# Decode attention and MLP on one core: weight products in VectorE and ScalarE loops, 451 TensorE instructions for 812, one load per contiguous 8 MB

## The chip, the cores and the metric

The kernel runs on one core of one Trainium2 chip. The metric is the device time of one execution in microseconds. Runs of one kernel agree closely: the kernel before took 1303.3, 1303.55 and 1303.74 us.

## What is computed

One decode step for one token: a layer norm, attention of 32 query heads over 8 cached key/value heads with 65536 keys each, a ReLU MLP beside it, and their sum with the input. All arrays are float32. The caches hold 2 x 268 MB, the weights 24 MB; each byte is read once.

```python
D, Hq, Hkv, Sk, Dh, Dff = 512, 32, 8, 65536, 128, 1792
xn = _layernorm(x, axis=-1)
q = (xn @ wq) as 32 heads of 128
scores = einsum("bhqd,bhkd->bhqk", q, repeat(k, 4)) * Dh ** -0.5
o = einsum("bhqk,bhkd->bhqd", softmax(scores), repeat(v, 4))
return x + o.reshape(1, 1, 4096) @ wo + relu(xn @ w1) @ w2
```

## The kernel before

**Loads.** SyncE (SP) issues all the large loads on one queue, in this order: wq in two pieces (4 and 28 slices; a slice is 128 x 512 floats, 256 KB) into the buffer `vs`, then 64 loads of 8.4 MB each, keys into `ks` and values into `vs` by turns (k0 v0 k1 v1 ... k31 v31), then w1 and w2 into `ks`, then wo in seven pieces into `vs`. There is one buffer each for keys and values. So k(i+1) is issued when the scores of step i have left `ks` (semaphore `k_free`, L297 behind L375), and v(i+1) when the weighted sum of step i has left `vs` (`v_free`, L302 behind L398). The first value load waits until TensorE has read wq out of `vs` (L310). In HBM the 128 rows of such a load, 64 KB each, lie 256 KB apart for keys and values alike; w1 and w2 are read in whole contiguous arrays.

**Head.** VectorE makes the layer norm, with two small matmuls that sum over partitions (L202 to L222). TensorE multiplies 32 slices of wq by selectors of x into one PSUM bank (L280); a copy, four transposes and a sum give the queries `qall`. GpSimd (POOL) copies four of them at a time to `qcur`.

**Steps.** 32 steps (8 heads of 4). In each, TensorE makes scores of 16384 keys with 32 matmuls (L344), VectorE transposes them from PSUM (L376), takes a running maximum (L385 to L393), ScalarE exponentiates (L422), and TensorE sums values by weights with 32 matmuls (L360). VectorE adds that to `acc` with the correction `alpha` (L400 or L402). A float32 matmul stands as two weight loads and two matmuls in the records. After four steps VectorE folds the head into `fin` (L408 to L415), and POOL copies it to `fins`.

**Tail.** After the last step TensorE multiplies w1 (L443), collects the heads (L453, L458), and transposes; VectorE builds the weights `hT` and `sw` (L460 to L494). TensorE then multiplies 14 slices of w2 and 28 of wo into four rows of `acc_z` (L505), as they land. `rows` takes `acc_z` (L536). The last four slices of wo go straight to `acc_y` (L540), `rows` is added there (L525), VectorE transposes (L552), and SP writes the 512 results (L561).

**Names.** `Flow.op` adds a wait and a semaphore increment to an instruction; the wait is then an instruction of its own only where it is not carried by the operation. `load_slices` issues one load for each count in a list. `nc.Fori` is a loop run by the engine's own sequencer, without unrolling. `mark_branch_hint_location` and `branch_hint` place a branch prefetch hint: before, on VectorE.

Of the kernel before, what the change touches and what calls it, by code (L numbers as in the profile page):

```python
# [15 lines left out]
P = 128  # L16
# [9 lines left out]
CHUNK = SK  # L26
# [3 lines left out]
NP = TPC // NT  # L30
# [6 lines left out]
WQ = [4, 28]  # L37
WO = [8, 8, 8, 4, 2, 1, 1]
PAIRED = 16
DIRECT = 28  # L40
# [29 lines left out]
def attention_and_mlp_kernel(  # L70
# [35 lines left out]
    def bank(name, *shape):  # L106
        return nc.alloc_psum_tensor(name, [P, *shape], F32).ap()

    ks = place("ks", NT * KEYS)
    vs = place("vs", NT * KEYS)  # L110
    tr = place("tr", NT * SUB, 32)
    wt = place("wt", NT * SUB, G)
    xT, xc, sq, xn = (place(n, A) for n in ("xT", "xc", "sq", "xn"))
    x4, yt = place("x4", P), place("yt", 32, 4)
    sw = place("sw", SLICES)
    mine = place("mine", HKV)
    octet = place("octet", P)
    eighth = place("eighth", R)

    flat_tr = tr.rearrange("p b i -> p (b i)")  # L120
    xs = flat_tr[:, : SLICES * HKV].rearrange("p (i h) -> p i h", h=HKV)
    xm = flat_tr[:, SLICES * HKV : SLICES * (HKV + 1)]
    om, spread = flat_tr[:, : R * HQ], flat_tr[:, R * HQ : 2 * R * HQ].rearrange("p (r h g) -> p r h g", r=R, h=HKV)
    heads = flat_tr[:, 2 * R * HQ : 2 * R * HQ + 2 * DH]
    st = place("st", 8)
# [4 lines left out]
    qall, qcur = place("qall", HKV, G), place("qcur", 32)  # L130
# [7 lines left out]
    acc, masked = place("acc", WIDE, DH), place("masked", WIDE, DH)  # L138
    fin, fins = place("fin", DH + G), place("fins", HKV, DH + G)
    rows = place("rows", 512)  # L140
    total, oT, hT = place("total", HQ), place("oT", HQ), place("hT", 4 * CT)

    pa, pb = bank("pa", 2, TW), bank("pb", 2, TW)
    acc_o, acc_z, acc_y, pm = (bank(n, 512) for n in ("acc_o", "acc_z", "acc_y", "pm"))

    names = "k_in v_in tiles scores m_out bias_out a_out w_out o_out k_free v_free q_in d_out f_out f_free"
    (
        k_in, v_in, s_tiles, s_dve, s_max, s_bias, s_alpha, s_w, s_o,
        k_free, v_free, q_in, s_diff, f_out, f_free,
    ) = (nc.alloc_semaphore(n) for n in names.split())  # L150
    PE, DV, AC, GP = (Flow(nc, e, n) for e, n in ((te, "pe"), (ve, "dve"), (se, "act"), (ge, "pool")))
# [6 lines left out]

    def load_slices(name, src, counts):
        marks = []  # L160
        for n in counts:
            cut = slice(len(marks) * D, (len(marks) + n) * D)
            marks += [load(sy, f"{name}{len(marks)}", vs[:, cut], src[:, cut])] * n
        return marks


    with tc.tile_critical():
        x_in = load(se, "x_in", xT, x.rearrange("(p a) -> p a", p=P))
        wq_in = load_slices("wq", wq.rearrange("h (i r) a f -> (h i) (r a f)", r=R), WQ)
        sy.dma_start(ks, k[0, 0, :, : NT * KEYS]).then_inc(k_in, 16)  # L170
# [4 lines left out]
    make_identity_marks = []  # L175

# [3 lines left out]
    d = memset(DV, ones, 1.0)  # L180
    d = memset(DV, x4, 0.0)
    x4_free = DV.mark
    d = memset(DV, qcur, 0.0)
    for t in (acc_o, acc_z, pm):
        memset(DV, t, 0.0)
    memset(DV, acc_y[:, :P], 0.0)

# [9 lines left out]
    x4_in = None  # L197
    se.wait_ge(*x4_free)
    x4_in = load(se, "x4_in", x4[0:P:32, :], x.rearrange("(c n) -> c n", c=CT))


    DV.op(lambda e: e.reduce_sum(st[:, 0:1], xT, axis=AX.X), x_in)  # L202
    PE.op(lambda e: e.matmul(pm[:, 0:1], ones, st[:, 0:1], start=True, stop=True), DV.mark)
    DV.op(lambda e: e.tensor_scalar_mul(st[:, 1:2], pm[:, 0:1], 1.0 / D), PE.mark)
    DV.op(lambda e: e.tensor_scalar(xc, xT, st[:, 1:2], None, op0=ALU.subtract), DV.mark)
    DV.op(lambda e: e.tensor_mul(sq, xc, xc), DV.mark)
    DV.op(lambda e: e.reduce_sum(st[:, 2:3], sq, axis=AX.X), DV.mark)
    PE.op(lambda e: e.matmul(pm[:, 1:2], ones, st[:, 2:3], start=True, stop=True), DV.mark)
    DV.op(
        lambda e: e.tensor_scalar(st[:, 3:4], pm[:, 1:2], 1.0 / D, EPS, op0=ALU.mult, op1=ALU.add),  # L210
        PE.mark,
    )
# [3 lines left out]
    AC.op(lambda e: e.activation(alpha[:, 0:1], st[:, 3:4], AF.Exp))  # L216
# [5 lines left out]
    xn_in = DV.op(lambda e: e.tensor_scalar_mul(xn, xc, st[:, 7:8]), DV.mark)  # L222
# [14 lines left out]
    DV.op(lambda e: e.reduce_sum(mine, ident.rearrange("p (h i) -> p h i", h=HKV), axis=AX.X))  # L237
    DV.op(lambda e: e.reduce_sum(eighth, ident.rearrange("p (i r) -> p r i", r=R), axis=AX.X))
    DV.op(lambda e: e.reduce_sum(octet[:, : P // R], ident.rearrange("p (i r) -> p i r", r=R), axis=AX.X))
    DV.op(  # L240
        lambda e: e.tensor_copy(
            octet[:, P // R :].rearrange("p (h i) -> p h i", i=P // R),
            octet[:, : P // R].unsqueeze(1).to_broadcast([P, HKV - 1, P // R]),
        ),
        DV.mark,
    )
    DV.op(
        lambda e: e.tensor_mul(
            xm.rearrange("p (r a) -> p r a", a=A),
            eighth.unsqueeze(2).to_broadcast([P, R, A]), xn.unsqueeze(1).to_broadcast([P, R, A]),  # L250
        )
    )
    pz = pb[:, 1, :]
    PE.op(lambda e: e.matmul(pz[:, :SLICES], octet, xm, start=True, stop=True), DV.mark)
    xs_in = DV.op(
        lambda e: e.tensor_mul(
            xs, pz[:, :SLICES].unsqueeze(2).to_broadcast([P, SLICES, HKV]),
            mine.unsqueeze(1).to_broadcast([P, SLICES, HKV]),
        ),
        PE.mark,  # L260
    )
    DV.op(lambda e: e.memset(idg, 1.0))
    DV.op(lambda e: e.tensor_copy(idg[:, :G], ident[:G, :G]), DV.mark)

    pr, pt = pa[:, 0, :], pb[:, 0, :]

    def turn():

        for j in range(4):
            PE.op(  # L270
                lambda e: e.transpose(pt[:, j * P : (j + 1) * P], rows[:, j * P : (j + 1) * P], ident),
                DV.mark, made,
            )
        return pt.rearrange("p (j c l) -> p j c l", j=4, c=CT)

    cleared = DV.op(lambda e: e.memset(pr, 0.0))
    for i in range(SLICES):
        c = i % CT
        PE.op(
            lambda e: e.matmul(  # L280
                pr[32 * c : 32 * c + HKV, :], xs[:, i, :], vs[:, i * 512 : (i + 1) * 512],
                start=(i < CT), stop=(i >= SLICES - CT),
            ),
            cleared, xs_in, wq_in[i],
        )
    wq_read = PE.mark
    DV.op(lambda e: e.tensor_copy(rows, pr), PE.mark)
    q = turn()[:, :, :, :HKV].rearrange("p j c h -> p h j c")
    DV.op(lambda e: e.reduce_sum(qall, q, axis=AX.X), PE.mark)
    q_made = DV.mark  # L290
    PE.need(DV.mark)
    AC.need(DV.mark)


    def k_load(h, n):
        sy.wait_ge(k_free, 1).then_inc(k_free, -1)
        sy.dma_start(ks, k[h, 0, :, n * NT * KEYS : (n + 1) * NT * KEYS]).then_inc(k_in, 16)  # L297

    def v_load(h, n):
        sy.wait_ge(v_free, 1).then_inc(v_free, -1)  # L300
        src = v[h].rearrange("(p t b) d -> p t (b d)", p=P, b=SUB)
        sy.dma_start(vs, src[:, n * NT : (n + 1) * NT, :].rearrange("p t f -> p (t f)")).then_inc(v_in, 16)  # L302

    def head(h):
        v_load(h, 0)
        for n in range(1, NP):
            k_load(h, n)
# [285 lines left out]
```

## Time and profile before

| | |
|---|---|
| median of 3 runs | 1303.55 us |
| profiled execution, its own time | 1303.26 us |
| span of its instructions | 1301.9 us |
| what lies around the span | 1.36 us |
| busy: TensorE / VectorE / ScalarE | 664.9 / 268.4 / 76.0 us |
| moved by DMA | 561.06 MB |

The span begins with the first instruction and ends with the last. Lines "L344" are line numbers of the kernel. In a timeline the columns are start, duration, engine, line, operation, output<-inputs, count, and in brackets how long the engine stood idle before and what released it. In a table of groups they are the shape, the count, total busy time and mean ns of one, then idle time before. "SPq" is SP's queue, that is an instruction that issues a DMA or waits; "PEq" and "DVEq" are the same of TensorE and VectorE. Register, branch and semaphore instructions have no rows.

### The profile page before, as it was taken

The page shows a single profiled execution, that of the slowest core. Times are in us where ns is not written, and L with a number is a line of the kernel's source. Part 1 is how long each engine was busy: PE and PEld are TensorE (multiplying, and loading weights), DVE is VectorE, ACT ScalarE, POOL GpSimd, SP SyncE. Part 2 cuts the span into 40 slices and gives each one's busy share as a digit, 9 for nine tenths or more (in the row PEclk, how much of TensorE's full clock was granted, in tenths as well). Part 3 has the DMA queues.
Part 4 walks back from the last instruction along what each step waited for, and adds up shares of the span by engine and source line. Part 5 has one row for each costly group of instructions (what it writes and reads, how often), then busy time and mean ns, then how long its engine had stood idle before and what let it go on. Part 6 is the DMA issues. An engine that isn't in the chain of part 4 may idle for free. (4 is left out here: it accounts for less than half of the span.)

```text
span 1301.9 us, 10665 instructions
## 1 busy us (share of the span) xinstructions
PE 664.9 (51%) x4512; PEld 185.6 (14%) x4512; DVE 268.4 (21%) x398; ACT 76.0 (6%) x292; POOL 4.1 (0%) x22
## 2 busy tenths in 40 slices
PE   3355356455446445545545545544544644544658
PEld 1111111111111111111111111111111111111112
DVE  2221122221122222012222012222112222201222
ACT  0000000000000000000000000000000000000000
POOL 0000000000000000000000000000000000000000
PEclk9776676777677677667677677768777767767769
DMA  9999999999999999999999999999999999999998
GB/s 419 419 449 419 451 419 445 425 427 443 421 449 421 449 419 451 419 445 425 431 439 425 445 421 449 419 451 419 445 425 435 435 425 445 421 449 421 449 416 361
DMA packets 11101, 561.06 MB, mean 431 GB/s; under 512 B 1492, under 2 KB 1496, under 8 KB 1880
## 3 DMA queue, kind: packets, MB, share of 16 engines
q1 hardware_dynamic: 10944, 561.00, 99.7%
q8 instruction: 3, 0.05, 0.0%
q10 hardware_dynamic: 152, 0.00, 0.0%
q14 instruction: 2, 0.02, 0.0%
HBM read 560.99 MB, written 0.00 MB: 431 GB/s over the span
## 5 line engine op out<-in xcount | busy, mean ns | idle before, releaser
L360 PE MATMUL acc_o<-vs,wt 128*16 128x512 f32 x2048 | 296.3, 743 | 179.0 <-PEq L356 179.0
L344 PE MATMUL pa<-ks,qcur 128*32 128x512 f32 x1024 | 176.5, 822 | 323.8 <-PEq L339 323.8
L376 DVE STREAM_TRANSPOSE tr<-pa 128x1024 f32<-128x1024 f32 x64 | 80.0, 1250 | 412.9 <-PE pa L344 412.9
L344 PE MATMUL pb<-ks,qcur 128*32 128x512 f32 x1024 | 139.5, 665 | 0.0
L422 ACT ACTIVATE wt<-tr,bias 128x128 f32<-128x128 f32 x128 | 64.3, 511 | 1084.5 <-ACTq L420 1084.5
L360 PEld LDWEIGHTS acc_o<-vs,wt 128*16 128x16 f32 x2048 | 69.6, 114 | 379.0 <-issue 379.0
L344 PEld LDWEIGHTS pa<-ks,qcur 128*32 128x32 f32 x1024 | 38.9, 134 | 431.4 <-issue 422.4
L402 DVE SCALAR_TENSOR_TENSOR acc<-acc,alpha,acc_o 128x512 f32<-128x512 f32 x24 | 17.9, 747 | 353.2 <-PE acc_o L360 353.2
L376 DVE STREAM_TRANSPOSE tr<-pb 128x1024 f32<-128x1024 f32 x64 | 80.0, 1250 | 49.6 <-PE pb L344 49.6
L344 PEld LDWEIGHTS pb<-ks,qcur 128*32 128x32 f32 x1024 | 41.9, 132 | 107.8 <-issue 88.6
L349 PE MATMUL pm<-ident,m 128*4 128x128 f32 x32 | 10.3, 320 | 87.7 <-DVE m L388 67.2
L400 DVE COPY acc<-acc_o 128x512 f32<-128x512 f32 x8 | 5.5, 692 | 121.5 <-PE acc_o L360 121.5
L350 PE MATMUL pm<-dg,ones 4*128 4x4 f32 x64 | 15.4, 309 | 21.4 <-DVE dg L392 21.4
L385 DVE TENSOR_REDUCE mc<-tr 128x4 f32<-128x512 f32 x24 | 24.1, 1006 | 1.8
L422 ACT ACTIVATION_READ_ACCUMULATOR wt<-tr,bias 128x1 f32 x128 | 23.9, 187 | 0.0
L349 PEld LDWEIGHTS pm<-ident,m 128*4 128x4 f32 x32 | 2.6, 81 | 116.7 <-DVE m L388 89.0
L350 PEld LDWEIGHTS pm<-dg,ones 4*128 4x128 f32 x64 | 12.6, 245 | 29.0 <-DVE dg L392 29.0
L351 PE MATMUL pm<-dg,rowg 4*128 4x1 f32 x64 | 14.7, 296 | 0.0
L280 PE MATMUL pa<-vs,tr 128*8 128x512 f32 x64 | 9.6, 754 | 8.7 <-DMA vs<-wq 7.4
L351 PEld LDWEIGHTS pm<-dg,rowg 4*128 4x128 f32 x64 | 13.4, 258 | 0.0
L390 DVE TENSOR_REDUCE mg<-pm 4x1 f32<-4x128 f32 x32 | 8.9, 279 | 13.2 <-PE pm L349 13.2
L505 PE MATMUL acc_z<-vs,sw 128*1 128x512 f32 x56 | 10.1, 592 | 2.1 <-DMA vs<-wo 2.1
(98 smaller groups left out, 97.8 us busy)
## 6 DMA issues: line engine op xcount, KB each, us to landing
vs<-wq SPq DMA_DIRECT2D x1, 7168.0 KB, 21.3
ks<-w SPq DMA_DIRECT2D x2, 3584.0 KB, 22.4
vs<-wo SPq DMA_DIRECT2D x3, 2048.0 KB, 16.4
vs<-wq SPq DMA_DIRECT2D x1, 1024.0 KB, 4.8
vs<-wo SPq DMA_DIRECT2D x1, 1024.0 KB, 22.8
ks<-k SPq DMA_DIRECT2D x32, 28.8
vs<-v SPq DMA_DIRECT2D x32, 28.9
vs<-wo SPq DMA_DIRECT2D x1, 512.0 KB, 23.6
```

The source lines that it names most:

```text
L280: lambda e: e.matmul(pr[32 * c : 32 * c + HKV, :], xs[:, i, :], vs[:, i * 512 : (i + 1) * 512], start=(i < CT), stop=(i >= SLICES - CT),),
L344: i = te.matmul(tile_of[32 * c : 32 * c + 32, :], qcur, ks[:, at : at + TW], start=True, stop=True)
L349: te.transpose(pm[:G, :P], m, ident)._wait_ge(s_dve, 3).then_inc(s_max, 1)
L350: te.matmul(pm[:, P : P + G], ones[:G, :], dg[:, :G], start=True, stop=True)._wait_ge(s_dve, 4)
L351: te.matmul(pm[:, P + G : P + G + 1], rowg, dg[:, G : G + 1], start=True, stop=True).then_inc(s_max, 1)
L360: mm = te.matmul(acc_o[32 * c : 32 * c + WIDE * G, :], wt[:, i * WIDE : (i + 1) * WIDE, :].rearrange("p b g -> p (b g)"), vs[:, i * 512 : ...
L376: i = ve.transpose(tr[:, s * SUB : (s + 2) * SUB, :].rearrange("p b i -> p (b i)"), (pa, pb)[s // 2 % 2].rearrange("p i k -> p (i k)"),)._ ...
L385: i = ve.reduce_max(top, tr[:, :, :G].rearrange("p b g -> p g b"), axis=AX.X)
L390: ve.reduce_max(mg, pm[:G, :P], axis=AX.X)._wait_ge(s_max, 1)
L402: ve.scalar_tensor_tensor(flat, flat, alpha[:, n : n + 1], acc_o, op0=ALU.mult, op1=ALU.add)
L422: i = se.activation(wt[:, :, g], tr[:, :, g], AF.Exp, bias=bias[:, n, g : g + 1], scale=scale, accum_out=part[:, n, g : g + 1],)
L505: lambda e: e.matmul(acc_z[32 * c : 32 * c + 1, :], lhsT, row, start=c not in begun, stop=last),
```

## The change

- **Layout.** `CHUNK` is 16384 keys instead of 65536. The 128 rows of each key or value load now lie back to back in HBM, 8.4 MB contiguous. Packet sizes stay 64 KB. SP's loads are one loop of 31 turns.
- **Head.** wq comes in two pieces of 16 slices; w1 is loaded right behind wq into a buffer of its own, ahead of the keys. The layer norm runs on 16 partitions with VectorE transposes instead of matmuls. wq is multiplied by VectorE, one slice per turn of a loop of 32 turns (L265 to L270): two waits, an address made in registers, and a SCALAR_TENSOR_TENSOR `accq = slice * xs + accq` that waits for the one before it through the semaphore `own`. One matmul with `mine` sums it per head. Then VectorE multiplies w1 in four instructions of 1792 elements (L315 to L322), and four matmuls and a transpose give the hidden values `hs`. TensorE waits for them (L334) ahead of the loop of steps. The first value load waits for the end of the wq loop (`q_dve`, L346).
- **Steps.** As before. In the fourth step of a head what does not need the last sum is folded ahead of it (L449 to L461). ScalarE, VectorE and POOL share one loop over heads.
- **Tail.** The last value load is split in two (21 and 11 of its 32 slices). Behind it come w2 in two pieces and wo in eight, `[9, 7, 5, 5, 3, 1, 1, 1]`; the first two pieces of wo fit in `ks` and need no `v_free`. Slices 0 and 1 of w2 are added by VectorE ahead of the loop; slices 2 to 39 of w2 and wo are taken in a loop of 19 turns, in which ScalarE scales an even slice and TensorE sums it over partitions, and VectorE adds an odd slice to `accy`. Slices 40 to 42 are matmuls into `acc_z`. `rows` is `accy + acc_z`; the last three slices go to `acc_y`.
- **TensorE's code.** 451 instructions instead of 812, and a branch prefetch hint ahead of its loop of steps, whose branch stands in a block that is never entered. VectorE's hint is gone.

```diff
-CHUNK = SK
+CHUNK = SK // 4
...
+    for n in range(2):
+        ge.wait_ge(*wq_in[n * SLICES // 2]).then_inc(go_dve, SLICES // 2)
...
+    with nc.Fori(0, SLICES, engines=[ENG.DVE]) as t:
+        ve.wait_ge(go_dve, 1).then_inc(go_dve, -1)
+        ve.wait_ge(own, 1).then_inc(own, -1)
+        ve.scalar_tensor_tensor(
+            accq, vs[:, bass.ds(t * D, D)], xs[:, bass.ds(t, 1)], accq, op0=ALU.mult, op1=ALU.add
+        ).then_inc(own, 1)
+    ve.wait_ge(own, 1).then_inc(q_dve, 1)
...
-    for i in range(SLICES):
-        c = i % CT
...
+    for a in range(A):
+        w = t1[:, a * DFF : (a + 1) * DFF]
+        if a == 0:
+            DV.op(lambda e: e.tensor_scalar_mul(h1, w, xn[:, 0:1]), DV.mark, w1_in)
+        else:
+            DV.op(
+                lambda e: e.scalar_tensor_tensor(h1, w, xn[:, a : a + 1], h1, op0=ALU.mult, op1=ALU.add), DV.mark
...
     PE.need(DV.mark)
...
+    sy.wait_ge(q_dve, 1)
     sy.sem_inc(v_free, 1)
+    with nc.Fori(0, STEPS - 1, engines=[ENG.SP]) as i:
+        v_load(i)
+        k_load(i + 1)
+    sy.wait_ge(v_free, 1).then_inc(v_free, -1)
+    sy.dma_start(vs[:, :LATE], v_parts[STEPS - 1][:, :LATE]).then_inc(v_in, 16)
+    sy.dma_start(vs[:, LATE:], v_parts[STEPS - 1][:, LATE:]).then_inc(v_late, 16)
     sy.wait_ge(k_free, 1)
...
-    w1_in = load(sy, "w1_in", t1, w1.rearrange("p a f -> p (a f)"))
-    w2_in = load(sy, "w2_in", t2, w2.rearrange("p j n -> p (j n)"))
+    w2_in = load_slices("w2", t2, w2.rearrange("p j n -> p (j n)"), [FB // 2, FB // 2])
...
+    with nc.Fori(0, TURNS, engines=[ENG.Activation, ENG.PE, ENG.DVE]) as t:
...
+        se.wait_ge(go_act, 1).then_inc(go_act, -1)
+        se.activation(even, even, AF.Copy, scale=scale_e).then_inc(go_pe, 1)
+        te.wait_ge(go_pe, 1).then_inc(go_pe, -1)
+        te.matmul(acc_z[:1], ones[:, 0:1], even, start=False, stop=False)
+        ve.wait_ge(go_dve, 1).then_inc(go_dve, -1)
+        ve.wait_ge(own, 1).then_inc(own, -1)
+        ve.scalar_tensor_tensor(accy, odd, scale_o, accy, op0=ALU.mult, op1=ALU.add).then_inc(own, 1)
...
+    z_in = PE.mark
+    ve.wait_ge(own, 1)
+    folded = DV.op(lambda e: e.tensor_add(rows, accy, acc_z), z_in)
```

The order of the instructions shows the change at two places on VectorE and one on SP. The first is VectorE between the layer norm and the loop of steps. Before, what stands there is set-up, the clearing of a bank, and the two small copies of the queries (`rows`, `qall`):

```order
L256 TENSOR_TENSOR tr<-pb,mine 128x256
L262 MEMSET idg 4x5
L263 COPY idg<-ident 4x4
L276 MEMSET pa 128x512
L287 COPY rows<-pa 128x512
L289 TENSOR_REDUCE qall<-pb 128x32
```

Now the loop over wq (L265; ISA is the instruction that makes the address) and the products with w1 (`tr<-t`, L318 and L321) stand there too. First the loop and the copies of the queries behind it:

```order
L265 UNCONDITIONAL_BRANCH
L268 ISA
L268 SCALAR_TENSOR_TENSOR acc<-kv,xs,acc 128x512
L265 REGISTER_ALU
L265 COMPARE_AND_BRANCH
L275 COPY rows<-pa 8x512
L281 COPY qall<-pb 128x32
```

That is the wq product, which has moved here from TensorE as a loop. Some rows further on VectorE, ahead of its own loop over heads (L400):

```order
L318 TENSOR_SCALAR tr<-t,xn 128x1792
L321 SCALAR_TENSOR_TENSOR tr<-t,xn,tr 128x1792 x3
L330 STREAM_TRANSPOSE tr<-pm 128x448
L332 TENSOR_SCALAR hs<-tr 128x14
L400 UNCONDITIONAL_BRANCH
```

The w1 product has moved here from TensorE's tail.

The second place is VectorE after the last head. Before, it prepares the weights, copies `acc_z` once and transposes:

```order
L468 RECIPROCAL total<-pm 128x32
L469 COPY hT<-pb 128x16
L471 TENSOR_TENSOR oT<-pa,total 128x32
L479 TENSOR_TENSOR tr<-eighth,oT 128x256
L487 TENSOR_TENSOR tr<-pb,mine 128x256
L494 TENSOR_REDUCE sw<-tr 128x32
L536 COPY rows<-acc_z 128x512
```

Now two slices stand ahead of the weights, and the loop of 19 turns behind them, with one register instruction more per turn than the loop over wq:

```order
L483 SCALAR_TENSOR_TENSOR accy<-kv,hs,accy 128x512 x2
L496 STREAM_TRANSPOSE tr<-pb 128x256
L497 RECIPROCAL total<-pm 128x32
L499 TENSOR_TENSOR per<-total,mine 128x32
L504 TENSOR_REDUCE inv<-per 128x4
L506 TENSOR_TENSOR hs<-tr,inv 128x32
L525 UNCONDITIONAL_BRANCH
L535 ISA
L535 REGISTER_ALU
L535 SCALAR_TENSOR_TENSOR accy<-kv,hs,accy 128x512
L525 REGISTER_ALU
L525 COMPARE_AND_BRANCH
```

Slices of w2 and wo that TensorE took straight from the buffers now pass through VectorE, which was nearly free there.

The third place is SP's queue at its start, as the difference of the two:

```order
-L155 DMA vs<-wq 128x2048
-L155 DMA vs<-wq 128x14336
-L170 DMA ks<-k 128x16384
+L165 DMA kv<-wq 128x8192 x2
+L165 DMA t<-w 128x7168
+L183 DMA kv<-k 128x16384
```

The load of w1 (`t<-w`, 3.7 MB) has moved from behind the last step to ahead of the first keys.

477 lines of the change are left out of this document (235 added, 242 removed).

## The prediction

> **What bounds the kernel now.** I read the page first, for its DMA rows.
>
> ```profile
> span 1301.9 us, 10665 instructions
> q1 hardware_dynamic: 10944, 561.00, 99.7%
> q8 instruction: 3, 0.05, 0.0%
> ```
>
> Read as queue, kind, packets, MB and share: SP's queue keeps the 16 DMA engines busy 99.7% of the span. So the kernel is one long read of 561 MB, and its time is when the read starts, how fast it goes, what interrupts it, and what follows its end. SP's timeline and the table by windows show the first three (last columns of the table: TensorE's clock, DMA share, GB/s).
>
> ```profile
> 0.97 0.86 SPq L155 DMA_DIRECT2D vs<-wq  x2
> 1.89 0.42 SPq L170 DMA_DIRECT2D ks<-k  x1
> 31.11 0.35 SPq L302 DMA_DIRECT2D vs<-v  x1
> 51.82 0.34 SPq L297 DMA_DIRECT2D ks<-k  x1
> ...
> 1233.09 0.33 SPq L302 DMA_DIRECT2D vs<-v  x1
> 1252.96 0.81 SPq L155 DMA_DIRECT2D ks<-w  x2
> ```
> ```profile
> 34.00:1250.00 1216.00, 615.30 (x4163) 172.46 (x4167) 248.67 (x339) 70.52 (x278) 2.92 (x14) 0.72 1.00 434
> 1260.00:1276.00 16.00, 12.96 (x96) 3.20 (x96) 2.76 (x6) 0.21 (x1) 0.12 (x1) 0.74 0.99 426
> 1297.00:1298.00 1.00, 1.00 (x8) 0.10 (x8) 0.00 (x0) 0.00 (x0) 0.00 (x0) 1.00 0.59 211
> ```
>
> From the first value load (31.11) to the last (1233.09) are 62 loads in 1201.98 us: 19.39 us for 8.39 MB, 433 GB/s. At that rate 561 MB take 1296 us; the read thins out in 1297 to 1298 (211 GB/s), so it ran from about 2.0, some 1.05 us behind the first issue. Each buffer is refilled about 10 us before the other load has ended (issues alternate every 20 us, a load is through one load later), so nothing interrupts it. What follows its end stands in the chain of waits:
>
> ```profile
> 1263.04 9.74 PE acc_o L360 x64
> ...
> 1272.81 0.03 DVEq L398
> ...
> 1300.07 0.41 DVE yt L552
> ```
>
> Only the first 2 us and the last 4 are not reading. The bytes stay the same. So the change can gain little, and loses where VectorE starves the read or is still working when the read is over.
>
> **The change part by part.** *One turn of VectorE's loop.* Two terms hang on it.
>
> ```profile
> 51.69 1.25 DVE L376 STREAM_TRANSPOSE tr<-pb 128x1024 f32<-128x1024 f32 x1 [0.58 <-PE pb L344]
> ...
> 1253.02 1.25 DVE L376 STREAM_TRANSPOSE tr<-pb 128x1024 f32<-128x1024 f32 x1 [0.58 <-PE pb L344]
> ...
> 1272.92 0.75 DVE L402 SCALAR_TENSOR_TENSOR acc<-acc,alpha,acc_o 128x512 f32<-128x512 f32 x1 [15.54 <-PE acc_o L360]
> 1273.74 0.17 DVE L408 TENSOR_TENSOR diff<-bias 128x12 f32<-128x12 f32 x1
> 1273.83 0.68 DVE L409 TENSOR_TENSOR masked<-acc,selb 128x512 f32<-128x512 f32 x1
> ```
>
> The same operation takes 0.75 us with one operand in PSUM; within SBUF the nearest row, the product L409, takes 0.68. Turns cannot overlap: each waits for the last through `own`, in an instruction of its own. What that costs: TensorE ends at 1272.78 (1263.04 + 9.74), the wait L398 stands at 1272.81, the operation starts at 1272.92, so 0.14. Between wait and operation now stands the making of the address. No row shows that on VectorE; on SP one does. The transposes at 51.69 and 1253.02 stand behind the same wait (L375) that lets SP load. The key load with an address in registers left 0.13 after its transpose (51.82), the fixed load of w1 0.06 before it (1252.96), so the address cost 0.19. A turn lies between 0.68 (all else hidden) and 0.75 + 0.14 + 0.19 = 1.08 with one register instruction, 1.18 with two. I take 0.10 for each, since the standing wait, an instruction of the same sequencer, costs 0.14 with its signal: **0.99 us** for wq, **1.08** in the tail. Counting and branching come behind the operation, and its 0.75 hides them; uncovered they would cost 0.1 to 0.3.
>
> *Head.*
>
> ```profile
> vs<-wq SPq DMA_DIRECT2D x1, 1024.0 KB, 4.8
> ```
> ```profile
> L400 DVE COPY acc<-acc_o 128x512 f32<-128x512 f32 x8 | 5.5, 692 | 121.5 <-PE acc_o L360 121.5
> ...
> L463 DVE COPY tr<-pb 128x256 f32<-128x256 f32 x1 | 0.4, 424 | 0.2 <-PE pm L458 0.2
> ```
> ```profile
> 30.69 0.69 DVE L287 COPY rows<-pa 128x512 f32<-128x512 f32 x1 [17.26 <-PE pa L280]
> ...
> 32.57 0.19 POOL L328 COPY qcur<-qall 128x4 f32<-128x4 f32 x1 [28.46 <-DVE qall L289]
> ```
>
> wq's first 1.05 MB landed at 5.8 (0.97 + 4.8), so 4.2 MB land at 13.1. The layer norm, some 25 small operations at 0.2 (L408: 0.17) and a few fills, is over by then. 32 turns of 0.99 end at 44.8; the second half of wq is there at 22.8, so VectorE sets the pace. v0 is issued at 45, and wq, w1 and k0 (20.45 MB) flow until 49.2: no gap yet. Then one chain: a matmul 0.7 and the copy and transposes to the queries (32.57 - 30.69 = 1.9), to 47.4; a dozen constants at 0.2 and a matmul, 3.3, to 50.7; w1. An element costs (692 - 424) / 256 = 1.05 ns, so 1792 cost 2.03 in the first operation and 2.09 in the other three, 8.4 with the waits, to 59.1; four matmuls 0.9, a transpose of 448 columns 0.55 (1.25 for 1024), a small operation and waits, to 60.8. The constants and w1 were hidden in keys' time before; here the scores of step 0 wait for them. k1 is issued 9.3 later (1252.96 against TensorE's start at 1243.69, below), at 70.1, and flows from 71.2. v0 is through at 49.2 + 19.4 = 68.6. The read stands still for **2.6 us**. In general the gap is 32 T - 29.1 for a turn T: nothing up to 0.91, and 5.5 at 1.08. Later steps close up: v1 is needed at 90.6 and `vs` is free near 87.
>
> By the Trainium skill, "VectorE: DVE Perf Modes", section "Mode 2×_2P", a float32 tensor_scalar within SBUF gives two results per cycle. By that rule the first w1 operation would cost about 0.9 us less and the gap would be 1.7. No row here shows such an operation of that length.
>
> *Steps.* Same loads and same TensorE work. A head is folded a little earlier, hidden as the next keys land after it. Nothing; if that cover went, about 1 us per head.
>
> *Tail.*
>
> ```profile
> 1243.69 1.08 PE L344 MATMUL pa<-ks,qcur 128*32 128x512 f32 x4 [10.78 <-PEq L339]
> 1279.84 6.18 PE L505 MATMUL acc_z<-ks,hT 128*1 128x512 f32 x28
> ```
> ```profile
> 1259.01 0.51 ACT L422 ACTIVATE wt<-tr,bias 128x128 f32<-128x128 f32 x1
> 1259.41 0.19 ACT L422 ACTIVATION_READ_ACCUMULATOR wt<-tr,bias 128x1 f32 x1
> 1259.50 0.28 ACT L428 ACTIVATE alpha<-bias 128x1 f32<-128x1 f32 x1
> ```
> ```profile
> 1274.77 1.06 DVE L415 TENSOR_REDUCE fin<-masked 128x128 f32<-128x512 f32 x1
> ...
> 1277.22 0.42 DVE L463 COPY tr<-pb 128x256 f32<-128x256 f32 x1 [0.22 <-PE pm L458]
> ```
>
> With w1 gone ahead, the last keys land 3.67 MB / 433 = 8.5 us later (the gap comes on top). Weights at 1259.6 + 8.5 = 1268.1, weighted sum at 1277.8 (9.74). The two parts of the last values land near 1265 and 1271.5, ahead of TensorE: the split costs and gains nothing. VectorE: product 0.68, sum 1.06, addition 0.3, drains and wait 0.4, to 1280.2. POOL and TensorE took 1.4 from there to L463 (1275.83 to 1277.22); with POOL's address, and TensorE in part at half clock after its pause, 2.0, to 1282.2. A transpose, a reciprocal and three small operations 1.35, and the loop's start: first turn near 1283.8. 19 turns end at 1283.8 + 18 x 1.08 + 0.75 = 1304.0. The slices are there sooner: slice 39 lands about 1296. ScalarE's Copy has no row; between 0.28 (one element) and 1.2 (by the slope to 0.51 for 128), 19 are over by 1304 at the latest. TensorE needs 6.18 / 14 = 0.44 a slice, twice that at half clock. So VectorE is last. Then the addition with its wait 0.84, and two groups of matmuls 0.8 to 1.5: the transpose starts near 1305.9 instead of 1300.07, **5.8 us** late. It would be on time at T = 0.76, and is 7.6 late at 1.18.
>
> *TensorE's code.* q8 has three packets of 16 KB, each 0.6 us of one DMA engine (433 / 16 = 27 GB/s). The ragged end of the read (211 GB/s) is a few late engines. Fewer such packets can end the read 0 to 1.8 us sooner; I take nothing, since VectorE's lateness hides it. The hint runs once, ahead of TensorE's loop, for 0.1 us at most as a register instruction, in the time of the first keys.
>
> **Sum**: 1303.26 (span and 1.36 around it) + 2.6 + 5.8 = 1311.7. The median lies 0.3 above the profiled run: **1312.0**.
>
> **Rivals.** *The turns keep up*: T at or under 0.76 as sequencer work is hidden; no gap, an end as before or up to 1.5 earlier, 1302 to 1303.5. For it, the lower bound of 0.68; against it, `own` stands ahead of the address in the order. *In between*, T 0.85 to 0.95: no gap or 1 us, 1.7 to 3.5 late, 1305 to 1308. *Faster*: contiguous rows speed up the read itself. 0.1 us off each of 62 loads is 6 us, 1297, once the turns keep up as well. Against it: w1 and w2, contiguous already, went at 426 GB/s where the strided loads have 434. The Trainium skill, "DMA: Bandwidth & Descriptors", section "Latency and other measured facts", has copies slowed by large power-of-two row pitches; at this pitch of 256 KB the trace speaks against it. *It doesn't do what it says*: code is still fetched in the tail; same time, VectorE being last.
>
> **How the numbers follow.** Forecast's mechanism (T over 0.95) 0.62, in between 0.12, the turns keep up 0.22, faster 0.04. Within 0.2%, about what a measurement of this kernel can tell from no change, is 1300.9 to 1306.2: the turns that keep up and half of those in between, 0.28. Slower 0.68, faster 0.04. The range reaches down to the turns that keep up, 1302, and up to both upper bounds, 1303.6 + 5.5 + 7.6 = 1316.7, say 1316.5. The forecast's own range is 1307 to 1316.5.
>
> **What would show it.** Right: L268's turns 0.95 to 1.05 apart and L535's 0.1 more; scores of step 0 near 61, k1 issued past 69; `rows` waiting for VectorE when wo landed us before. Wrong: turns under 0.8, scores of step 0 before 58, or `rows` waiting for a DMA.

## The result, and the profile after

The changed kernel takes **1316.54 us** (median of 6 runs, 1315.24 to 1318.04); the kernel before took 1303.41 (6 runs, 1303.3 to 1303.74). The ratio is 1.0101, with a 95% interval of 1.0088 to 1.0114: 13.1 us slower. The profiled execution took 1316.53 us, with a span of 1315.2. Of all the runs below one, of the version with a small load ahead of the last write, took 2098 us and is left out of its ratio.

The page first, span and SP's queue (packets, MB, share of 16 engines):

```profile
span 1315.2 us, 11218 instructions
q1 hardware_dynamic: 11376, 561.00, 98.8%
```

The same 561 MB, but the DMA engines are no longer busy to the end: 98.8% where it was 99.7%. The table by windows says where the reading is missing (the last columns are TensorE's clock, DMA share and GB/s; the rows are the time around the first scores, and the steps). Before:

```profile
66.00:76.00 10.00, 6.13 (x56) 1.38 (x46) 0.69 (x1) 0.00 (x0) 0.00 (x0) 0.95 0.98 426
100.00:1250.00 1150.00, 585.83 (x3961) 163.73 (x3965) 234.47 (x321) 66.16 (x261) 2.92 (x14) 0.72 1.00 433
```

After:

```profile
66.00:76.00 10.00, 6.75 (x60) 2.02 (x52) 6.50 (x7) 0.00 (x0) 0.00 (x0) 1.00 0.55 210
100.00:1250.00 1150.00, 566.89 (x3954) 158.69 (x3946) 247.08 (x341) 68.37 (x270) 2.94 (x14) 0.74 1.00 433
```

The steps read at 433 GB/s in both. Between 66 and 76 the rate is half: (426 - 210) x 10 / 426 = **5.1 us of reading are missing**. Two shorter windows of the changed kernel show that the read stands still there and is not merely slow:

```profile
68.00:70.00 2.00, 2.00 (x24) 0.53 (x16) 1.53 (x2) 0.00 (x0) 0.00 (x0) 1.00 0.00 0
70.00:72.00 2.00, 2.00 (x24) 0.53 (x16) 1.36 (x2) 0.00 (x0) 0.00 (x0) 1.00 0.00 0
```

The timeline of the changed kernel there shows the chain that leads to it (start, duration, engine, line, operation):

```profile
13.93 0.75 DVE L268 SCALAR_TENSOR_TENSOR acc<-kv,xs,acc 128x512 f32<-128x512 f32 x1 [0.67 <-DVEq L267]
14.97 0.75 DVE L268 SCALAR_TENSOR_TENSOR acc<-kv,xs,acc 128x512 f32<-128x512 f32 x1 [0.28 <-DVEq L267]
...
45.90 0.75 DVE L268 SCALAR_TENSOR_TENSOR acc<-kv,xs,acc 128x512 f32<-128x512 f32 x1 [0.28 <-DVEq L267]
46.77 1.88 PE L274 MATMUL pa<-acc,mine 128*8 128x512 f32 x2 [31.59 <-DVEq L271]
47.16 0.34 SPq L343 DMA_DIRECT2D kv<-v  x1
...
52.97 1.15 DVE L318 TENSOR_SCALAR tr<-t,xn 128x1792 f32<-128x1792 f32 x1
54.16 6.33 DVE L321 SCALAR_TENSOR_TENSOR tr<-t,xn,tr 128x1792 f32<-128x1792 f32 x3
60.54 1.67 PE L326 MATMUL pm<-tr,ones 128*1 128x448 f32 x8 [8.29 <-DVE tr L321]
...
63.83 3.25 PE L373 MATMUL pa<-kv,qcur 128*32 128x512 f32 x16 [1.61 <-PEq L368]
...
72.57 0.34 SPq L339 DMA_DIRECT2D kv<-k  x1
```

32 turns stand (45.90 - 13.93) / 31 = 1.031 us apart, each with 0.28 idle ahead of it that ends with the sequencer's own wait (DVEq L267). The queries, the constants and w1 follow one after another, the scores of step 0 start at 63.83, and k1 is issued at 72.57, after v0 is through.

The end of the timeline, from the last weighted sum on:

```profile
1273.23 9.54 PE L391 MATMUL acc_o<-kv,wt 128*16 128x512 f32 x64 [2.56 <-PEq L385]
...
1289.63 0.75 DVE L535 SCALAR_TENSOR_TENSOR accy<-kv,hs,accy 128x512 f32<-128x512 f32 x1 [0.44 <-POOLq L522]
1290.75 0.75 DVE L535 SCALAR_TENSOR_TENSOR accy<-kv,hs,accy 128x512 f32<-128x512 f32 x1 [0.36 <-DVEq L534]
...
1309.55 0.75 DVE L535 SCALAR_TENSOR_TENSOR accy<-kv,hs,accy 128x512 f32<-128x512 f32 x1 [0.35 <-DVEq L534]
1310.33 0.69 DVE L546 TENSOR_TENSOR rows<-accy,acc_z 128x512 f32<-128x512 f32 x1
1311.08 0.61 PE L551 MATMUL acc_y<-rows,ones 128*1 128x128 f32 x8 [5.21 <-DVE rows L546]
...
1312.25 0.41 DVE L572 STREAM_TRANSPOSE yt<-acc_y 128x128 f32<-128x128 f32 x1 [1.23 <-PE acc_y L551]
1312.69 0.34 SPq L165 DMA_DIRECT2D y<-yt  x1
```

Here the turns are (1309.55 - 1289.63) / 18 = 1.107 us apart, and TensorE stands idle for 5.21 us until VectorE has `rows`. The transpose comes 12.2 us later than before (1300.07). A third piece stands in the table of DMA issues (last number: median us from issue to landing), before and after:

```profile
y<-yt SPq DMA_DIRECT2D x1, 2.0 KB, 1.4
```
```profile
y<-yt SPq DMA_DIRECT2D x1, 2.0 KB, 2.5
```

The last write takes 1.1 us longer. So 13.3 us between the two profiled executions are 5.1 in the head, 7.1 in the tail (12.2 - 5.1) and 1.1 in the last write.

### The profile page after: what moved, and what is told of

It is laid out like the page before. It is cut to its first block, busy times and chain, and to the rows that moved or that the text cites. A ratio compares the mean times of both kernels' runs of the same rounds, so it can differ in the third digit from the quotient of the medians.

```text
span 1315.2 us, 11218 instructions
## 1 busy us (share of the span) xinstructions
PE 639.4 (49%) x4362; PEld 177.8 (14%) x4362; DVE 327.2 (25%) x477; ACT 89.6 (7%) x311; POOL 6.4 (0%) x27
## 3 DMA queue, kind: packets, MB, share of 16 engines
q1 hardware_dynamic: 11376, 561.00, 98.8%
## 5 line engine op out<-in xcount | busy, mean ns | idle before, releaser
L391 PE MATMUL acc_o<-kv,wt 128*16 128x512 f32 x2048 | 289.9, 730 | 182.3 <-PEq L385 182.3
L373 PE MATMUL pa<-kv,qcur 128*32 128x512 f32 x1024 | 173.4, 810 | 317.8 <-PEq L368 317.8
L373 PE MATMUL pb<-kv,qcur 128*32 128x512 f32 x1024 | 133.9, 640 | 0.0
L391 PEld LDWEIGHTS acc_o<-kv,wt 128*16 128x16 f32 x2048 | 68.4, 112 | 377.1 <-issue 377.1
L373 PEld LDWEIGHTS pa<-kv,qcur 128*32 128x32 f32 x1024 | 39.0, 134 | 425.0 <-issue 414.7
L466 DVE SCALAR_TENSOR_TENSOR acc<-acc,alpha,acc_o 128x512 f32<-128x512 f32 x16 | 12.0, 747 | 239.4 <-PE acc_o L391 239.4
L373 PEld LDWEIGHTS pb<-kv,qcur 128*32 128x32 f32 x1024 | 40.3, 127 | 102.4 <-issue 83.3
L268 DVE SCALAR_TENSOR_TENSOR acc<-kv,xs,acc 128x512 f32<-128x512 f32 x32 | 24.1, 752 | 9.3 <-DVEq L267 9.3
L274 PE MATMUL pa<-acc,mine 128*8 128x512 f32 x2 | 1.9, 1042 | 31.6 <-DVEq L271 31.6
L532 PE MATMUL acc_z<-kv,ones 128*1 x38 | 16.9, 603 | 0.0
L535 DVE SCALAR_TENSOR_TENSOR accy<-kv,hs,accy 128x512 f32<-128x512 f32 x19 | 14.3, 752 | 6.8 <-DVEq L534 6.0
```

Of the source, the lines that this page charges most:

```text
L268: ve.scalar_tensor_tensor(accq, vs[:, bass.ds(t * D, D)], xs[:, bass.ds(t, 1)], accq, op0=ALU.mult, op1=ALU.add).then_inc(own, 1)
L373: i = te.matmul(tile_of[32 * c : 32 * c + 32, :], qcur, ks[:, at : at + TW], start=True, stop=True)
L391: mm = te.matmul(acc_o[32 * c : 32 * c + WIDE * G, :], wt[:, i * WIDE : (i + 1) * WIDE, :].rearrange("p b g -> p (b g)"), vs[:, i * 512 : ...
L466: ve.scalar_tensor_tensor(flat, flat, alpha[:, n : n + 1], acc_o, op0=ALU.mult, op1=ALU.add)
L532: te.matmul(acc_z[:1], ones[:, 0:1], even, start=False, stop=False)
L535: ve.scalar_tensor_tensor(accy, odd, scale_o, accy, op0=ALU.mult, op1=ALU.add).then_inc(own, 1)
```

## The experiments

**Each loop written out.** VectorE's 32 products of wq as 32 instructions, the wait for the one before carried by the product:

```diff
-    with nc.Fori(0, SLICES, engines=[ENG.DVE]) as t:
-        ve.wait_ge(go_dve, 1).then_inc(go_dve, -1)
-        ve.wait_ge(own, 1).then_inc(own, -1)
-        ve.scalar_tensor_tensor(
-            accq, vs[:, bass.ds(t * D, D)], xs[:, bass.ds(t, 1)], accq, op0=ALU.mult, op1=ALU.add
-        ).then_inc(own, 1)
...
+    for t in range(SLICES):
+        DV.op(
+            lambda e: e.scalar_tensor_tensor(
+                accq, vs[:, t * D : (t + 1) * D], xs[:, t : t + 1], accq, op0=ALU.mult, op1=ALU.add
+            ),
+            DV.mark, wq_in[t],
+        )
...
```

> The changed kernel with the 32 products of wq written out one by one on VectorE (fixed addresses, the wait for the one before carried by the operation) instead of a loop of 32 turns. Nothing else changes. Theory: the read stands still for 5.0 us because the loop's turns are 1.03 us apart; written out they are about 0.79 apart, the queries come 32 x 0.24 = 7.7 us sooner, k1 is issued near 64.9 instead of 72.57, ahead of the end of v0's transfer at 68, so no gap: 5.0 us less, 1311.5 (1310.5 to 1312.5); the tail moves up by 5.0 and keeps its length. Rival A, the turns are slow because the loads write into the same memory while VectorE reads it: still 1.03 apart, 1316.5. Rival B, the gap hangs on something behind the loop (constants, w1): the turns get shorter, k1 is still issued past 70, 1315 to 1316.5.

Measured: 1311.99 us (5 runs), 1.0064 of before (1.005 to 1.0078); 4.6 us less than the changed kernel. From its timeline and its table by windows:

```profile
13.35 25.16 DVE L265 SCALAR_TENSOR_TENSOR acc<-kv,xs,acc 128x512 f32<-128x512 f32 x32
...
64.91 0.34 SPq L339 DMA_DIRECT2D kv<-k  x1
```
```profile
66.00:76.00 10.00, 5.62 (x29) 1.71 (x33) 1.67 (x4) 2.09 (x8) 0.00 (x0) 0.68 0.97 419
```

32 products stand as one block: (25.16 - 0.75) / 31 = 0.787 apart. The turns are no longer 1.03 apart while the loads go on, so rival A falls. k1 is issued at 64.91, and the read goes on at 419 GB/s where it had 210; so rival B falls too.

The tail's 19 products in the same way, ScalarE and TensorE keeping their loop:

```diff
-    with nc.Fori(0, TURNS, engines=[ENG.Activation, ENG.PE, ENG.DVE]) as t:
+    with nc.Fori(0, TURNS, engines=[ENG.Activation, ENG.PE]) as t:
...
+    for j in range(FIRST + 1, end, 2):
+        DV.op(
+            lambda e: e.scalar_tensor_tensor(
+                accy, kv[:, j * D : (j + 1) * D], hs[:, j : j + 1], accy, op0=ALU.mult, op1=ALU.add
+            ),
+            DV.mark, arrivals[j],
+        )
...
```

> The changed kernel with VectorE's 19 products of the tail written out (fixed addresses) instead of in the loop; ScalarE and TensorE keep their loop of 19 turns, the loop over wq stays. Theory: the end waits for 19 turns 1.105 apart; at 0.79 apart they end at 1289.6 + 18 x 0.79 + 0.75 = 1304.6 instead of 1310.3, 5.7 us less: 1310.8, and 1309.7 if the write of y, issued sooner after the last load, takes 1.4 again and not 2.5. Rival A, the slices land too late for VectorE: the products get gaps that wait for a DMA and end past 1307, 1313 or more. Rival B, ScalarE and TensorE then end last: TensorE's loop ended at 1304.8 here, so rows waits for TensorE, and the gain is 5.3 at most, with rows waiting for acc_z.

Measured: 1312.06 us, 1.0067 (1.0053 to 1.0081); 4.5 us less, where 5.7 was expected. Its timeline:

```profile
1290.12 14.93 DVE L532 SCALAR_TENSOR_TENSOR accy<-kv,hs,accy 128x512 f32<-128x512 f32 x19
...
1306.55 0.69 DVE L546 TENSOR_TENSOR rows<-accy,acc_z 128x512 f32<-128x512 f32 x1 [1.50 <-PE acc_z L540]
```

VectorE is through at 1305.05, and now waits 1.50 for TensorE (`acc_z`): rival B holds. Both together:

> Both loops of VectorE written out. Theory: the two terms are independent and add: 5.0 + 5.7 less, 1305.8, or 1304.7 with the write of y at 1.4. Rival: other parts of the change cost time too (contiguous loads, a shared loop of ScalarE, VectorE and GpSimd, the split last load): then it stays above 1307. A second rival: the whole slowdown is elsewhere and the loops are hidden: 1315 or more.

Measured: 1306.72 us (9 runs), 1.0024 (1.0014 to 1.0034); 9.8 us less, and 0.9 more than the 1305.8 expected. The two gains add, as far as the spread of the runs can tell (4.6 + 4.5 = 9.1). Its timeline:

```profile
1281.58 17.68 PE L529 MATMUL acc_z<-kv,ones 128*1 x36
...
1301.08 0.69 DVE L546 TENSOR_TENSOR rows<-accy,acc_z 128x512 f32<-128x512 f32 x1 [2.55 <-PE acc_z L540]
```

`rows` waits 2.55 for TensorE. A slice of the loop is two matmuls, all into one row of `acc_z`; 36 in 17.68 are 0.98 us a slice, with waits for ScalarE and the transfers in them. Behind VectorE's loop stood a second one that was nearly as late. y is issued at 1303.02, 2.5 later than before (1300.51), and the write of y takes 2.4 instead of 1.4: together the 3.5 us by which this version is still slower than before.

**The hidden values ahead of step 0.** One product of w1 instead of four, loops as they are:

```diff
-    for a in range(A):
+    for a in range(1):
         w = t1[:, a * DFF : (a + 1) * DFF]
```

> The changed kernel with one of the four products of w1 (it leaves out three quarters of the MLP's first product). The loops stay as they are. Theory: the scores of step 0 wait for the hidden values, so 6.3 us less of VectorE ahead of them is 6.3 us off the chain, more than the gap of 5.0: k1 is issued near 66.2, no gap, 1311.5 (1310.5 to 1312.5). Rival: the read stops because v0 is issued late (47.2 instead of 31.1), which this leaves as it is: 1316.5.

Measured: 1310.97 us, 1.0057 (1.0044 to 1.0071); 5.6 less. Its timeline has v0 and k1 here, and its table by windows has the read:

```profile
46.96 0.34 SPq L343 DMA_DIRECT2D kv<-v  x1
...
67.44 0.34 SPq L339 DMA_DIRECT2D kv<-k  x1
```
```profile
66.00:76.00 10.00, 4.19 (x29) 1.56 (x25) 3.62 (x6) 2.09 (x8) 0.00 (x0) 0.68 0.98 419
```

v0 is issued as late as ever (46.96), yet the read does not stop. So the gap comes from the length of the chain up to k1: two parts of it were shortened, one at a time, and either ends the gap.

**The layout alone**, on the kernel before:

```diff
-CHUNK = SK
+CHUNK = SK // 4
...
-        sy.dma_start(ks, k[h, 0, :, n * NT * KEYS : (n + 1) * NT * KEYS]).then_inc(k_in, 16)
+        sy.dma_start(ks, k[h, n]).then_inc(k_in, 16)
```

> The kernel before with one part of the change alone: keys and values laid out so that each 8.4 MB load is contiguous (rows of 64 KB back to back instead of 256 KB apart). Theory: the read goes at the same rate, 62 loads in 1202 us, so 1303.3 (1303.0 to 1303.7), ratio 1.000. Rival, contiguous rows are read faster: 0.1 us off each of 62 loads is 6 us, 1297. Rival the other way: the runs of the changed kernel lie up to 3 us apart and those of before 1.1; if the layout makes that, the runs of this one lie as far apart.

Measured: 1303.6 us (11 runs, 1303.31 to 1303.95), 1.0002 (0.9993 to 1.0011). Its steps:

```profile
100.00:1250.00 1150.00, 585.09 (x3957) 164.29 (x3961) 233.84 (x320) 66.15 (x261) 2.93 (x14) 0.71 1.00 433
```

433 GB/s, as with rows 256 KB apart. Both rivals fall: no gain, and no wider spread (0.6 us).

**What a turn consists of.** Three runs with the loop over wq kept as a loop. First, the wait carried by the product, so that the address is made ahead of it:

```diff
-        ve.wait_ge(own, 1).then_inc(own, -1)
         ve.scalar_tensor_tensor(
             accq, vs[:, bass.ds(t * D, D)], xs[:, bass.ds(t, 1)], accq, op0=ALU.mult, op1=ALU.add
-        ).then_inc(own, 1)
+        )._wait_ge(own, 1).then_inc(own, 1)
+        ve.sem_inc(own, -1)
```

> The changed kernel, loop over wq kept, with registers for the address; only the wait for the product before is carried by the product itself (and own is taken down behind it), so that the address is made ahead of that wait. Theory: the address hid behind nothing because it stood behind the wait; now it is made while the product before still runs, and a turn is 0.80 to 0.85 instead of 1.03; the gap goes, 1311.7. Rival: a sequencer that waits for its engine makes no address meanwhile: 0.98 to 1.03, 1315 to 1316.5.

Second, two sums with a semaphore each:

```diff
-    with nc.Fori(0, SLICES, engines=[ENG.DVE]) as t:
...
+    with nc.Fori(0, SLICES // 2, engines=[ENG.DVE]) as t:
+        for i, (to, done_to) in enumerate(((accq, own), (acc2, own2))):
...
+    ve.tensor_add(accq, accq, acc2).then_inc(own, 1)
```

> The changed kernel, loop over wq kept, standing wait and address as they are, but two slices a turn into two sums with a semaphore each (added at the end), so that a product waits for the one before the last and not for the last. Theory: wait and address are then done while the other sum's product runs, 0.76 to 0.80 a slice; the gap goes, 1311.7. Rival: the sequencer issues nothing while a product runs: still 1.03 less half the branch, 0.95 to 1.03, 1313.5 to 1316.5.

Third, a fixed address:

```diff
-            accq, vs[:, bass.ds(t * D, D)], xs[:, bass.ds(t, 1)], accq, op0=ALU.mult, op1=ALU.add
+            accq, vs[:, :D], xs[:, :1], accq, op0=ALU.mult, op1=ALU.add
```

> The changed kernel, loop over wq kept with its two waits, but every turn multiplies slice 0 (a fixed address; the other 31 slices of wq are left out). This measures what the address costs. Theory as predicted: the wait 0.14, the address 0.10, so turns of 0.89 to 0.93; by the 1.03 measured, 0.28 lies between products, so the address is 0.10 to 0.14 of it. The queries come 3.2 to 4.5 us sooner and the gap is 0.5 to 1.8: 1312 to 1313.5. Rival: the address costs nothing and the wait all 0.28: 1.03, 1316.5.

Measured: 1311.41 us (1.0061, 1.0046 to 1.0076), 1310.53 (1.0057, 1.0041 to 1.0072) and 1312.79 (1.0074, 1.0059 to 1.0089), four runs each. The products of the first, second and third in their timelines:

```profile
13.81 25.16 DVE L267 SCALAR_TENSOR_TENSOR acc<-kv,xs,acc 128x512 f32<-128x512 f32 x32 [0.54 <-DVEq L266]
```
```profile
14.36 0.75 DVE L272 SCALAR_TENSOR_TENSOR acc<-kv,xs,acc 128x512 f32<-128x512 f32 x1 [0.83 <-DVEq L271]
15.02 0.75 DVE L272 SCALAR_TENSOR_TENSOR masked<-kv,xs,masked 128x512 f32<-128x512 f32 x1
...
34.90 0.75 DVE L272 SCALAR_TENSOR_TENSOR masked<-kv,xs,masked 128x512 f32<-128x512 f32 x1
```
```profile
13.56 28.65 DVE L268 SCALAR_TENSOR_TENSOR acc<-kv,xs,acc 128x512 f32<-128x512 f32 x32 [0.45 <-DVEq L267]
```

The steps are 25.16 less 0.75 over 31 = **0.787**, (34.90 - 14.36) / 31 = **0.663**, and 28.65 less 0.75 over 31 = **0.900**. The rivals of all three fall; the second, expected at 0.76 to 0.80, is shorter than a product itself. So a loop with registers and one carried wait is as fast as code written out (0.787 both): counting, branching, the wait for data and the address all hide behind the product that runs. What didn't hide is the standing wait and what stood behind it: the wait costs 0.900 - 0.787 = 0.113, the address 1.031 - 0.900 = 0.131. The 1.107 - 1.031 = 0.076 that the tail's turns take more is put down to their second register instruction; no run takes that away alone.

**Fewer turns in the tail**, loops as they were:

```diff
-TURNS = 19
+TURNS = 14
...
-                acc_z[32 * c : 32 * c + 1], hs[:, j : j + 1], kv[:, j * D : (j + 1) * D], start=(c != 0), stop=True
+                acc_z[32 * c : 32 * c + 1], hs[:, j : j + 1], kv[:, j * D : (j + 1) * D],
+                start=(c != 0 and j < end + CT), stop=(j >= gathered - CT),
```

> The changed kernel with 14 turns in the tail's loop instead of 19: ten slices go from the loop to TensorE's matmuls into four rows of acc_z. Both loops keep their form. Theory: VectorE has five turns of 1.105 less ahead of the end, 5.5 us, and nothing else is near: 1311.0 (1310 to 1312); the gap ahead of step 0 stays. Rival: TensorE, which gets the ten slices, ends last: 1313 or more, rows waiting for acc_z.

Measured: 1312.04 us, 1.0069 (1.0056 to 1.0083); 4.5 less. Its timeline:

```profile
1274.53 9.60 PE L391 MATMUL acc_o<-kv,wt 128*16 128x512 f32 x64 [2.55 <-PEq L385]
...
1305.34 0.75 DVE L535 SCALAR_TENSOR_TENSOR accy<-kv,hs,accy 128x512 f32<-128x512 f32 x1 [0.35 <-DVEq L534]
1306.13 0.69 DVE L547 TENSOR_TENSOR rows<-accy,acc_z 128x512 f32<-128x512 f32 x1
```

From the last weighted sum's start to `rows` it is 31.6 us, and 37.1 in the changed kernel: 5.5 less, five turns of 1.107. Against that, the weighted sum starts 1.3 later in this execution. VectorE is still last (`rows` starts right behind its last product), so the rival falls.

**Carried waits in both loops, and 14 turns:**

> Both loops of VectorE kept as loops with registers, but with the wait carried by the product (as in the run with the carried wait), and 14 turns in the tail. Theory: no gap (5.0), turns of 0.79 in the tail too, and TensorE, which ended last at 1300.97 in the run with both loops written out since its 19 turns of the loop cost 0.86 each, takes ten slices in four column groups instead of one: the end then follows the last slice of wo as in the kernel before, y is issued at 1300.5 to 1301.2, and with 2.4 for the write 1304.3 (1303.3 to 1305.3). Rival A: the two registers of the tail's address do not hide behind 0.75: turns of 0.85 to 1.0, still early enough, same time. Rival B: TensorE ends last all the same, past 1306.

Measured: 1305.2 us (11 runs), 1.0018 (1.0009 to 1.0027); 11.3 less than the changed kernel, and still 2.0 more than before. The profiled execution took 1304.62. Its timeline:

```profile
1282.82 12.21 PE L532 MATMUL acc_z<-kv,ones 128*1 x27
1284.63 11.00 DVE L534 SCALAR_TENSOR_TENSOR accy<-kv,hs,accy 128x512 f32<-128x512 f32 x14 [0.32 <-DVEq L533]
...
1294.86 4.02 PE L541 MATMUL acc_z<-kv,hs 128*1 128x512 f32 x23
...
1298.49 0.32 PEld L554 LDWEIGHTS acc_y<-kv,hs 128*1 128x1 f32 x8 [0.54 <-DMA kv<-wo]
1299.04 0.69 DVE L549 TENSOR_TENSOR rows<-accy,acc_z 128x512 f32<-128x512 f32 x1 [3.41 <-PE acc_y L554]
...
1300.98 0.34 SPq L165 DMA_DIRECT2D y<-yt  x1
```

With two registers the turns are (11.00 - 0.75) / 13 = 0.788 apart, so rival A falls. Of rival B half holds: `rows` waits 3.41 for TensorE, whose weight loads (PEld) wait there for slices of wo to land, but the median stays under 1306. TensorE's matmuls stand at 12.21 / 13.5 = 0.90 a slice in the loop, all in one row of `acc_z`, and at 4.02 / 11.5 = 0.35 behind it, in four rows. y is issued at 1300.98 (before: 1300.51). With 0.47 there and 0.9 more for the write, 1303.26 + 1.4 is the 1304.62 of this execution.

**The last write.** Three runs on this version: a small load just ahead of the write; no hint and no block for TensorE; the write issued by ScalarE.

```diff
+    sy.wait_ge(*folded)
+    warm = load(sy, "warm", place("spare", 32, rows=R * 2), x.rearrange("(i s) -> i s", s=32))
     sy.wait_ge(*DV.mark)
     done = load(sy, "y_out", out.rearrange("(p j) -> p j", j=4), yt[:, 0, :])
...
```

> The one before, with one more load: SP reads x (2 KB) into a tile of its own when rows is done, about 1.5 us ahead of the write of y. The write of y lands 1.4 us after its issue in the kernel before, where the last slice of wo lands 1.0 to 1.5 us ahead of it, and 2.2 to 2.6 in each changed one so far, where the queue has been quiet for 3.5 us and longer. Theory: a queue that has been quiet costs the 1.0; with a load just ahead y lands in 1.4 again and the time is 1.0 less than without it. Rival: the quiet isn't the cause, y takes 2.4 and the time is the same within 0.3; a second rival, y queues behind the load and lands up to 1 us later.

```diff
-    far = te.mark_branch_hint_location()
...
-    with nc.body("again", valid_engines=[ENG.PE]):
-        te.br_lt(turns, 1, on_true="again", on_false="over").branch_hint(far)
-    nc.switch_bb("over")
```

> The version with the wait carried in both loops and 14 turns, without TensorE's hint and the block that is never entered; nothing else changes. Theory: the hint costs one instruction ahead of TensorE's loop, in the time of the first keys, and changes nothing at the end: 1305.2 (1304.6 to 1305.8), y still 2.3 to 2.6 from issue to the wait that ends the program. Rival: the block switched to at the end of the program is what makes SP see y's semaphore late (the write's packets are done about 1.0 us after its issue before and after the change, SP's wait ends 0.4 us behind them before, 1.3 to 1.5 after): y takes 1.4 and the time is 1304.1. Second rival: without the hint TensorE fetches code in the tail, which lies on one DMA engine: up to 1 us more.

```diff
-    done = load(sy, "y_out", out.rearrange("(p j) -> p j", j=4), yt[:, 0, :])
+    done = load(se, "y_out", out.rearrange("(p j) -> p j", j=4), yt[:, 0, :])
...
```

> The same version (with the hint) with the write of y issued, and waited for, by ScalarE on its own queue instead of SP. If what is late is SP (its sequencer, or its queue behind 75 loads), y takes 1.4 from issue to the wait's end and the time is about 1304.1. Rival: the write itself or its completion is what is late, 2.3 to 2.6 whoever issues it, 1305.2.

Measured: 1305.78 us (1.0019, 1.0009 to 1.0028), 1305.44 (1.0018, 1.0009 to 1.0027) and 1305.48 (1.0021, 1.0012 to 1.003), that is the same as without each. The write's own row in the three tables of DMA issues, in the first with the small load's:

```profile
spare<-x SPq DMA_DIRECT2D x1, 2.0 KB, 2.4
y<-yt SPq DMA_DIRECT2D x1, 2.0 KB, 2.4
```
```profile
y<-yt SPq DMA_DIRECT2D x1, 2.0 KB, 2.4
```
```profile
y<-yt ACTq DMA_DIRECT2D x1, 2.0 KB, 2.4
```

Neither a quiet queue, nor the hint, nor SP makes the write late; the small load, of the same size, takes 2.4 as well. The hint and its block cost nothing that these runs can tell.

## Why the prediction was right in kind and short in size

The forecast was the right case: slower, by VectorE's turns, through a gap ahead of step 0 and a late tail. The median lies 0.04 us above the top of the range and 4.5 above the forecast: three terms of the sum were too small. Head and tail, 5.1 and 7.1, lie inside the bounds of 5.5 and 7.6 that the prediction added up to 1316.7 and then put at 1316.5; the last write, 1.1 more than before, was in no bound. That the head stayed inside is partly luck: its bound allowed for longer turns alone, the measured 1.031 gives 32 x 1.031 - 29.1 = 3.9 by the prediction's formula, and the other 1.2 are misses elsewhere in the chain that partly cancel. That the median lies just above the top and not just below is chance, since single runs differ by 2.8; that the sum was short is not. Point by point:

- **What bounds the kernel.** Right. The steps read at 433 or 434 GB/s in every kernel here, and the differences of several us lie ahead of step 1 and behind the last load.
- **One turn.** 0.99 and 1.08 forecast, 1.031 and 1.107 measured. The mechanism was right in its parts: the standing wait 0.113 (taken 0.14), the address 0.131 and, as far as the difference shows it, 0.076 (taken 0.10 each), and counting, branching and the wait for data hidden. What the sum lacked is the 0.035 that even written-out dependent products stand apart (0.787 against 0.752).
- **Head.** Forecast 2.6, measured 5.1: this term was mis-sized most. k1 was issued 2.5 us later than forecast (72.57 against 70.1). The loop began 0.8 later (13.93 against 13.1) and took 1.0 longer, so its end was 1.9 late (46.65 against 44.8). The matmul behind it took 1.88 instead of 0.7; the queries were 1.0 later for it, net of the copies. From the end of w1 to the scores it took 3.3 instead of 1.7, another 1.6, of which the four matmuls make 0.8 (1.67 instead of 0.9) and waits and small operations the rest. Against that, constants, w1 and the scores' own time were 0.6, 0.9 and 0.6 shorter. 1.9 + 1.0 + 1.6 - 2.1 = 2.4. The step that failed, the largest single miss of the sum, is the price of TensorE's matmuls in this chain: 0.7 and 0.9, for which the prediction shows no row, where 1.88 and 1.67 were measured. Passes of 512 columns took 12.21 / 27 = 0.45 each in the tail of the version with 14 turns and carried waits; here two took 1.88, after 31.6 us in which TensorE had stood idle. For the tail the prediction allowed TensorE half its clock after a pause, for the head it did not. That the lack of work ahead of these matmuls makes them slow is read from the traces; no run changed it alone.
- **Two results per cycle.** The first operation on w1 took 1.15 us for 1792 elements (L318), and the other three 2.1 each. The Trainium skill, "VectorE: DVE Perf Modes", section "Mode 2×_2P", which I had weighed and not taken, holds here: 0.9 us, as worked out there.
- **Steps.** Right: nothing.
- **Tail.** Forecast 5.8, measured 7.1. The weighted sum began at 1273.23, which is 1268.1 plus the gap of 5.1. The first turn came 16.4 behind it instead of 15.7, 18 turns took 19.9 instead of 19.4, and the rest 1.95 instead of 1.9. That VectorE is last, by five turns at least, is shown by the run with 14 turns. What I had not seen is how near the next one stood: TensorE's slices, taken at 0.44 to 0.9 each, took 0.98 with their waits in the run with both loops written out. The loop puts all of them into one row of `acc_z`; the row of before that I used spread them over four. The 0.90 in one row and 0.35 in four of the run with carried waits and 14 turns fit that, but no run changed the row alone.
- **The last write.** A step that failed too. The "span and 1.36 around it" of the sum carried the 1.4 us of before along without a reason, and it is 2.5. That is 1.1 us.
- **TensorE's code.** Taken at nothing. The changed kernel's page has no row for q8, which the prediction took for the fetching of TensorE's code. As far as that reading holds, the rival that the code is still fetched in the tail falls (three packets of q14, 0.02 MB, are left). What an earlier end of the read would bring, these runs don't show, since VectorE is last. In the version with 14 turns and carried waits one packet of q8 comes back, in the steps; without the hint a second one lies in the tail (1290 to 1303), and the time is the same.
- **Rivals.** The layout rival fell by its own run (1.0002). The Trainium skill, "DMA: Bandwidth & Descriptors", section "Latency and other measured facts", has copies between HBM tensors slow down with power-of-two row pitches from 512 KB (207 GB/s) up; no run here has such a pitch, and at 256 KB neither the steps' rate nor the time depends on the layout. "The turns keep up" is what the carried wait makes of the kernel: not far off, one instruction away.

In sum: 1311.7 + 2.5 (head) + 1.3 (tail) + 1.1 (write) = 1316.6.

**What stays open.** Why the write of y takes 2.2 to 2.6 us in every version of the changed kernel and 1.4 before (and 1.4 with the new layout alone). The three runs exclude causes and show none. The write's packets move within 1.2 us of its issue in both (1301.3 to 1301.7 before, 1313.5 to 1313.9 after); what has grown is the time from there to the end of the wait. The Trainium skill, "DMA: Bandwidth & Descriptors", section "Anatomy of one DMA — SWDGE (gpsimd) path", written for transfers that GpSimd issues, puts a fixed cost of some 2 us on one, most of it the confirmation of the write; 2.4 is near that, and 1.4 lies below it. Also open is the spread: the changed kernel's runs lie up to 2.8 us apart, those of before 0.4 to 1.1. The layout doesn't make it (0.6 there). The nine versions that read on at that place have their last weighted sums start anywhere from 1267.18 to 1269.24, the three with the full gap from 1273.23 to 1274.53, one execution each; so parts of head and tail are known to a microsecond or so, no better. That the changed tail starts from the landing of the last keys, and the old one's end from the end of the whole read, would explain the spread, but no run tried it.

## What to carry to other kernels

In a loop run by the engine, ask what stands behind a wait of its own: here that was paid in full each turn. With the wait carried by the operation it hid behind the operation that was running: 0.24 us of 1.03, from one instruction moved. When a loop on one engine is found to be last, look how late the next engine would be before putting a price on mending it; here the second kept the end 2.55 us late once the first was mended. And a kernel that reads memory all the time pays for any chain ahead of its first steady step once its buffers run dry: count that chain with the times of an engine that has hardly worked yet, not with those of one at work.

## What the runs showed of the hardware that was not expected

- Two products on VectorE that don't depend on each other overlap: 0.663 from start to start with 0.75 for each. With a dependency they are 0.787 apart.
- A loop with address registers costs VectorE nothing against code written out (25.16 us for 32 products in both) when the product carries its wait: the sequencer makes the next address while a product runs.
- After a pause of 31.6 us TensorE took 1.88 us for two passes of 512 columns (L274). The length of the pause is not all: two such passes ahead of the loop took 1.86 after 2.14 us (L272). The first 16 matmuls of step 0 took 3.25 us, the next 16 took 1.90. The profile gives the granted clock as 1.00 in these windows, so that column doesn't show it; in the kernel before, the first 16 matmuls of the last step took 3.64 us beside a granted clock of 0.50 (1243.7 to 1247.3).
